# Forward and backward of a gated mix of two attentions: query blocks asked for ten steps ahead, transposing loads issued a piece later, first tiles of a stage placed over tiles that are done early

## The chip, the cores and the metric

The kernel runs on one core of one Trainium2 chip. The metric is the device time of one launch in microseconds. Five engines carry the work: TensorE (PE in the profile; PEld is its weight load), VectorE (DVE), ScalarE (ACT), GpSimd (POOL) and SyncE (SP). SP, ACT and POOL also issue DMAs, each in the order of its own instruction queue, and the transfers run on 16 DMA engines.

## The reference

The kernel computes the output of a gated mix and the gradients of its inputs. Branch A is an attention with 32 query heads over one key and value head (2048 tokens, head size 18). Branch B goes through the same tokens in 64 segments of 32; each segment attends to itself and to 8 memory rows, and its output for these rows is the memory of the next segment.

```python
def _A_ref(x, wq, wk, wv, wo):                      # S=2048, D=576, H=32, Dh=18
    q = (x @ wq).reshape(B, S, H, Dh).transpose(0, 2, 1, 3)
    k, v = x @ wk, x @ wv
    p = softmax(einsum('bhqd,bkd->bhqk', q, k) * Dh ** -0.5)
    o = einsum('bhqk,bkd->bhqd', p, v)
    return o.transpose(0, 2, 1, 3).reshape(B, S, H * Dh) @ wo

def _B_ref(x, mem0, Wq, Wk, Wv, Wo, seg_len):       # H=32, Dh=128, M=8, seg_len=32
    mem = mem0
    for s in range(S // seg_len):
        h = concatenate([mem, x[:, s * seg_len:(s + 1) * seg_len]], axis=1)
        q, k, v = (einsum('btd,dhe->bhte', h, W) for W in (Wq, Wk, Wv))
        p = softmax(where(mask, einsum('bhqe,bhke->bhqk', q, k) * scale, -1e9))
        o = einsum('bhte,hed->btd', einsum('bhqk,bhke->bhqe', p, v), Wo)
        mem = o[:, :M]
        outs.append(o[:, M:])
    return concatenate(outs, axis=1)

g = sigmoid((x * gate_w).sum(-1, keepdims=True))
out = g * A(x) + (1 - g) * B(B_x)
# returned: out and the gradients of out, for a given grad_out, to the eleven inputs A_x ... gate_w
```

All inputs and outputs are bfloat16; B_x is a constant with no gradient.

## The kernel before, in words

The program is one long sequence of stages. Everything from the forward weave on is written with an order set by hand: within an engine, instructions run in the order in which the Python code emits them. The stages, with their stretch in the profiled execution (us from the span's start):

- projections, 0 to 432;
- the forward weave, 432 to 2138: the recurrent chain of B's forward (b_chain_fwd) with the steps of A's first pass (a_pass1) between its pieces;
- b_bulk, 2138 to 2770: the token part of B's backward that doesn't hang on the recurrence;
- the backward weave, 2770 to 4426: the recurrent chain of B's backward (b_chain_bwd, 64 segments, last one first) with the first 928 steps of A's second pass (a_pass2) between its pieces;
- b_post, 4426 to 4658: what is left of B's gradient to its inputs;
- b_dw, 4658 to 5422: weight gradients, with the last 96 steps of a_pass2 among them;
- a_final, 5422 to 5529.

**weave** (L279) runs 12 steps of a_pass2 first, then one piece of the chain and one step in turn, with some extra steps behind pieces 4, 7 and 9 (counted from the chain's start). Every fourth of the first 48 steps also loads a part of the weights WT (load_WT, tile WT, 1152 KB).

**a_pass2** (L1856): one step n recomputes a tile of A's scores (mm_S: b_S from b_KV and b_QS; ex: Exp on ACT into b_E), forms b_dP on PE, multiplies on DVE (b_dS) and accumulates into b_acc. Of step n + 1, mm_S and ex are emitted in step n; the accumulation of step n is emitted in step n + 1. The queries come from the DRAM buffer qs_dram, in blocks of four steps of 200 KB (128 partitions by QSW = 800 columns); a tile b_QS holds two of them (400 KB), there are two such tiles, and in step n with n % 8 == 1 the block pair n // 8 + 1 is loaded (L1874). In the backward weave these loads are issued by SP, in b_dw by ACT. At the end of the weave's share, b_acc is put by in part_dram (by way of the tile b_pto, which shares its buffers with b_E), and b_dw fetches it as b_prt.

**b_chain_bwd** (L994): 14 pieces for each segment. Loads for the next segment to come (s - 1) are emitted in the pieces of segment s: load_a (L1013 to L1019), load_b (r_kx and r_k, L1023 and L1025), load_c (L1028, L1030), load_dT (three transposing loads into the tile r_dT, L1035), and kv_load (r_kvS, r_kvR, r_ks, r_kr, L1069 to L1077). r_pj and r_x are PSUM tiles of its projections; WoT is the transposed output weight; dm is the memory's gradient.

**b_bulk**: in each tick (137 of them) trans() transposes four heads of q, k, dO, o and v on PE into a PSUM tile x_tr (two buffers) and copies it to SBUF (x_qT, x_kT ... L768). With q and k a second transposition rides along: transp() (L723) puts half of a tile of x_dS or x_P through PE into the same x_tr (copied at L755) and the other half through DVE's own transpose (L726), giving x_DT and x_PT, which later ticks read. x_po is the product that uses them, x_b another product.

**b_post** (L1264): 50 ticks; load() fetches y_ldk and y_ldv (L1295) or y_q, y_dO, y_pd, and y_dq by a transposing load (L1304); st_T transposes on PE (y_pt) into y_T, st_H accumulates y_pdx, and y_dx holds its result before the store to dxB_dram.

**b_dw** (L1388): load_h (L1421) fetches w_h, the other operand of the weight gradients, load(k) fetches w_d, two tiles for each k (L1410, 2 MB each, with transposing loads of oh_dram at L1414), and mem_tok fetches z_src (L588) and transposes z_v. w_acc holds the products.

SBUF pools are taken from the left or from the right (RIGHT); a tile that lies over another one's place waits until that one's last reader is done. Before, a_pass2's pools a3s and a3k are taken from the right in the weave; so are wH (for w_h) and yr behind it, while ys is on the left.

## Time and profile before

| | us |
|---|---|
| time, median of 3 runs | 5536.03 |
| the 3 runs | 5531.0, 5537.22, 5536.03 |
| time of the profiled execution | 5530.78 |
| its span | 5529.1 |
| PE busy, share of the span | 5202.2, 94% |
| mean granted clock of TensorE | 0.976 of full |

One execution was profiled. Each instruction has a start, a duration and, where its engine stood idle ahead of it, what ended the idle time (its releaser). Names such as b_S<-b_KV,b_QS say which tile an instruction writes and which it reads. In a window by stretch, the granted clock is the mean share of full speed that TensorE was given. A queue of DMA issues is named SPq or ACTq.

### The profile page before, as it was taken

How to read it: one execution, taken by the hardware profiler on the slowest of the kernel's cores; microseconds unless marked ns; L12 is line 12 of the kernel's file. 1: busy time of each engine (PE TensorE's matmuls, PEld its weight loads, DVE VectorE, ACT ScalarE, POOL GpSimd, SP SyncE). 2: the span in 40 equal slices, each digit the busy share in tenths (PEclk: the TensorE clock that was granted, in tenths of full speed). 3: DMA queues.
4: the chain of work that ended last, by engine and by line, in shares of the span. 5: the costliest groups of instructions: out<-in, count | busy, mean ns of one | idle time of the engine just before them, and what ended most of it. 6: DMA issues, size and time to landing. Idle time of an engine off the chain costs nothing. (4 is left out here: it accounts for less than half of the span.)

```text
span 5529.1 us, 221015 instructions
## 1 busy us (share of the span) xinstructions
PE 5202.2 (94%) x95713; PEld 2806.3 (51%) x95713; DVE 3576.1 (65%) x7083; ACT 3308.1 (60%) x4738; POOL 2163.1 (39%) x4186
## 2 busy tenths in 40 slices
PE   8999999999999998999979999999999988999998
PEld 6434444444444445666625455445555576754444
DVE  5337888888888887656668777777777812333322
ACT  4327788787878885555657777777777712222211
POOL 4004555554555544333324445444544411121112
PEclk9999999999999999999979999999999999999999
DMA  6646766766665546888765788787877687856653
GB/s 215 219 172 135 137 137 131 136 136 132 137 131 120 119 98 183 253 246 259 228 221 153 171 175 175 175 171 178 179 178 176 141 222 197 253 189 207 185 165 103
DMA packets 1030196, 959.11 MB, mean 173 GB/s; under 512 B 596834, under 2 KB 861931, under 8 KB 1019618
## 3 DMA queue, kind: packets, MB, share of 16 engines
q1 hardware_dynamic: 921730, 687.65, 52.5%
q0 software_dynamic: 100784, 247.24, 14.7%
q8 instruction: 748, 12.26, 1.0%
q10 hardware_dynamic: 6704, 10.08, 0.7%
q14 instruction: 230, 1.88, 0.1%
HBM read 522.08 MB, written 371.33 MB: 162 GB/s over the span
## 5 line engine op out<-in xcount | busy, mean ns | idle before, releaser
L1912 DVE TENSOR_TENSOR b_dS<-b_dP,b_E 128x512 bf16<-128x512 f32 x2048 | 1314.7, 684 | 586.5 <-PE b_dP L86 256.0
L1774 DVE TENSOR_TENSOR a_W<-a_dP,a_E 128x512 bf16<-128x512 f32 x2048 | 1314.4, 684 | 276.0 <-issue 128.3
L1888 ACT ACTIVATE b_E<-b_S 128x1024 bf16<-128x1024 f32 x1024 | 1048.7, 1024 | 629.3 <-PE b_dP L86 546.3
L1744 ACT ACTIVATE a_E<-a_S 128x1024 bf16<-128x1024 f32 x1024 | 1049.9, 1025 | 254.9 <-PE a_dP L86 168.1
L86 PEld LDWEIGHTS <-b_QS 32*128 32x128 bf16 (+1 forms) x8192 | 234.5, 89 | 586.8 <-issue 517.0
L86 PE MATMUL b_S<-b_KV,b_QS 32*128 32x512 bf16 x2048 | 412.3, 396 | 106.3 <-ACT b_E L1888 60.5
L86 PE MATMUL r_pj<-WT,r_dT 128*32 128x288 bf16 x12288 | 489.9, 290 | 5.2 <-issue 5.2
L86 PE MATMUL w_acc<-w_d,w_h 128*128 128x512 bf16 (+1 forms) x2400 | 484.6, 380 | 0.0
L86 PE MATMUL a_S<-a_QD,l_KV 32*128 32x512 bf16 x2048 | 399.5, 384 | 38.6 <-ACT a_E L1744 35.1
L86 PE MATMUL b_acc<-b_dS,b_QS 128*18 128x512 bf16 x2048 | 422.5, 396 | 2.2 <-issue 1.7
L86 PE MATMUL b_dP<-b_KV,b_QS 32*128 32x512 bf16 x2048 | 412.6, 398 | 1.5 <-DVE b_dS L1912 1.5
L86 PE MATMUL a_acc<-a_W,l_WK 128*32 128x512 bf16 x4096 | 413.6, 390 | 0.3 <-DVE a_W L1774 0.2
L86 PE MATMUL b_acc<-b_E,b_QS 128*18 128x512 bf16 x2048 | 409.4, 396 | 0.6 <-issue 0.6
L86 PE MATMUL a_acc<-a_E,l_VK 128*32 128x512 bf16 x4096 | 403.8, 381 | 4.8
L86 PE MATMUL a_dP<-a_QD,l_KV 32*128 32x512 bf16 x2048 | 399.4, 386 | 0.1
L86 PEld LDWEIGHTS <-r_dT 128*32 128x32 bf16 x12288 | 324.5, 97 | 99.4 <-issue 11.6
L86 PEld LDWEIGHTS <-w_h 128*128 128x128 bf16 (+1 forms) x2688 | 224.9, 100 | 257.8 <-issue 20.6
L86 PEld LDWEIGHTS <-hm 128*32 128x32 bf16 x7680 | 204.0, 97 | 194.8 <-issue 0.7
L869 POOL TENSOR_TENSOR x_prod<-x_dOT,x_oT 128x512 bf16<-128x512 bf16 x128 | 148.0, 1156 | 300.5 <-ACT x_oT L866 278.9
L86 PEld LDWEIGHTS <-l_KV 32*128 32x128 bf16 x4096 | 121.8, 91 | 249.7 <-issue 205.0
L86 PEld LDWEIGHTS <-l_WK 128*32 128x32 bf16 x4096 | 106.7, 93 | 221.1 <-issue 220.6
L86 PE MATMUL x_b<-WoN,x_oT 128*128 128x288 bf16 x1024 | 211.3, 290 | 3.5 <-issue 3.5
(465 smaller groups left out, 10118.2 us busy)
## 6 DMA issues: line engine op xcount, KB each, us to landing
b_QS<-qs_dram SPq DMA_DIRECT2D x116, 400.0 KB
dOx_dram<-p_tok SPq DMA_DIRECT2D x16, 1024.0 KB
c_vx<-vx_dram SPq DMA_DIRECT2D x64, 256.0 KB
krow_dram<-c_k POOLq DMA_DIRECT2D x64, 256.0 KB
qrow_dram<-c_q POOLq DMA_DIRECT2D x64, 256.0 KB
vrow_dram<-c_v POOLq DMA_DIRECT2D x64, 256.0 KB
x_q<-qx_dram SPq DMA_DIRECT2D x32, 512.0 KB
x_dO<-dOx_dram SPq DMA_DIRECT2D x32, 512.0 KB
```

The costliest lines, as they stand in the source:

```text
L86: return self.nc.tensor.matmul(out, lhsT, rhs, start=start, stop=stop, tile_position=tp, skip_group_check=True)
L869: nc.gpsimd.tensor_tensor(out=sc["prod", t][:], in0=sc["dOT", t][:], in1=oT[:], op=ALU.mult)
L1744: nc.scalar.activation(E_[n][:], S.pop(n)[:], ACT.Exp, scale=SCALEA)
L1774: nc.vector.tensor_tensor(out=W_[n][:, i, :], in0=dP[i][:], in1=E_[n][:, i, :], op=ALU.mult)
L1888: nc.scalar.activation(E_[n][:], S.pop(n)[:], ACT.Exp, scale=SCALEA)
L1912: nc.vector.tensor_tensor(out=D_[n][:, i, :], in0=dP[i][:], in1=E_[n][:, i, :], op=ALU.mult)
```

## The change

1. *Query blocks.* qs_dram is laid out by blocks of four steps. A tile b_QS holds one block (200 KB) and there are four of them, so they take the same room. Three are loaded at the start, and in step n with n % 4 == 1 block n // 4 + 3 is loaded. The store of qs_dram and its readers follow the new layout.
2. *Transposing loads of the chain.* load_dT(s - 1, 2) comes after load_b and after the next yield; load_dT(s - 1, 0) after the next yield. Two pieces of a segment so hand over to a step of a_pass2 before these loads are issued, and not after.
3. *b_bulk.* The DVE transpose of a ride is issued behind the two copies that read x_tr, and no longer ahead of them.
4. *Pools.* a3s and a3k are taken from the left, between rw and rs. In b_post, y_ldk and y_ldv come from ys (left) rather than yr (right), the two y_dx tiles are taken first in ys, and load(0) of dq is emitted ahead of load(1).
5. *w_h.* load_h is a method; b_post calls it in tick 31, where b_dw called it as its first act. In the queue order before, that call's loads were issued ahead of b_post's first ones.
6. *w_d.* For k == 0 the two tiles are taken in their plain order.

```diff
@@ -723,8 +723,7 @@
         def transp(d, r, nm, pt):
             self.tr(pt[:, 4, :], d[:, 1, r, :].rearrange("p i t -> p (i t)"), P)
             o = sp.tile([P, 256], BF16, name=nm, bufs=2)
-            nc.vector.transpose(o[:, 0:128], d[:, 0, r, :].rearrange("p i t -> p (i t)"))
-            return o
+            return o, d[:, 0, r, :].rearrange("p i t -> p (i t)")
 
         def attend_m(PT, m):
             po = psum.tile([P, 4, P], F32, name="x_po", bufs=2)
@@ -752,7 +751,8 @@
             if 0 <= t < NG:
                 trans_out(t, w, nb, pt)
             if o2:
-                nc.vector.tensor_copy(o2[:, 128:256], pt[:, 4, :])
+                nc.vector.tensor_copy(o2[0][:, 128:256], pt[:, 4, :])
+                nc.vector.transpose(o2[0][:, 0:128], o2[1])
 
         def trans_out(t, w, nb, pt):
             tt, g, r, d = view(t)
@@ -772,8 +772,9 @@
             def put(pt):
                 if 0 <= t < NG:
                     tt, g, r, d = view(t)
-                    sc[out, t] = transp(d[nm], r, "x_" + out, pt)
-                    return sc[out, t]
+                    o2 = transp(d[nm], r, "x_" + out, pt)
+                    sc[out, t] = o2[0]
+                    return o2
             return put
 
         st_QT = lambda t: trans(t, "q", 2, ride(t - 8, "dS", "DT"))
@@ -1199,11 +1200,11 @@
             yield
             mem_cols(1, mem_grad("r_x", ((rows(mrow["dx"]), [perm] * 8), (rows(mrow["q"]), blk(dSqB)))))
             heads(4)
-            load_dT(s - 1, 2)
             if s:
                 load_b(s - 1, nxt)
             nc.gpsimd.dma_start(self.dTm_dram[s // 16][:, :, s % 16, :], dTc[:].rearrange("p w u c t -> p w (u c t)"))
             yield
+            load_dT(s - 1, 2)
             heads(3)
             kv_mm(n0 + 1)
             yield
@@ -1214,12 +1215,12 @@
                 pad_in("p", nxt["pT"][:, 1, :])
             yield
             heads(8)
-            load_dT(s - 1, 0)
             if s:
                 Pq = pad_T("p")
             if n1 == 0:
                 kv_load(0)
             yield
+            load_dT(s - 1, 0)
             heads(6)
             if n1 - n0 == 4:
                 kv_mm(n0 + 2)
@@ -1261,7 +1262,14 @@
         nc.vector.tensor_copy(mg[:, :, P:GD], pt[0:8, 4, 0:64].rearrange("p (g c) -> p g c", c=16))
         nc.gpsimd.dma_start(self.outs[6].rearrange("b m d -> (b m) d"), m)
 
-    def b_post(self, sp, rp, psum):
+    def load_h(self, xs, ms, wH):
+        n = self.NTT + self.NM // P
+        ht = wH.tile([P, n, D], BF16, name="w_h", bufs=1)
+        self.nc.sync.dma_start(ht[:, 0:self.NTT, :], xs.rearrange("(n p) d -> p n d", p=P))
+        self.nc.sync.dma_start(ht[:, self.NTT:n, :], ms.rearrange("(n p) d -> p n d", p=P))
+        return ht
+
+    def b_post(self, sp, rp, psum, wH):
         nc = self.nc
         NTT = self.NTT
         T0 = self.T - RIDE * (self.NSEG - KR)
@@ -1291,7 +1299,7 @@
                 names = [{"q": "dk", "dO": "dv"}.get(w, w) for w in names if w != "pd"]
             for w in names:
                 if w in ("dk", "dv"):
-                    d[w] = rp.tile([P, 8, P], BF16, name=f"y_l{w}", bufs=3)
+                    d[w] = sp.tile([P, 8, P], BF16, name=f"y_l{w}", bufs=3)
                     nc.sync.dma_start(d[w][:].rearrange("p h e -> p (h e)"),
                                       self.xtok[w][tt * P:(tt + 1) * P, h0 * P:h0 * P + 1024])
                     continue
@@ -1352,16 +1360,17 @@
                         self.mm(pdx[tt][:, hf, 0:288], lhsT=d[w][:, i, :], rhs=self.WT[wi][:, 4 * g + i, 288 * hf:288 * hf + 288],
                                 start=(g == 0 and wi == 0 and i == 0), stop=(g == 7 and wi == 2 and i == 3))
             if g == 7:
-                dx = sp.tile([P, D], BF16, name="y_dx", bufs=2)
+                dx = dxt[tt % 2]
                 nc.scalar.copy(dx[:].rearrange("p (a b) -> p a b", a=2), pdx.pop(tt)[:, :, 0:288])
                 n = min(P, T0 - tt * P)
                 nc.gpsimd.dma_start(self.dxB_dram[tt * P:tt * P + n, :], dx[0:n, :])
 
         stages = (st_KV, st_T, st_H)
+        dxt = [sp.tile([P, D], BF16, name=f"y_dx{i}") for i in range(2)]
         load(0, ("pd", "q", "dO"))
+        load(0, ("dq",))
         load_s(0)
         load(1, ("pd", "q", "dO"))
-        load(0, ("dq",))
         load(2, ("pd", "q", "dO"))
         load(1, ("dq",))
         load(2, ("dq",))
@@ -1379,6 +1388,8 @@
             for n, st in enumerate(stages):
                 if 0 <= t - n < NG:
                     st(t - n)
+                if n == 0 and t == 31:
+                    self.ht = self.load_h(self.db_dram, self.dm_dram, wH)
                 if n == 0 and t < NG:
                     if t % 2 == 1:
                         load(t // 2 + 3, ("pd", "q", "dO"))
@@ -1406,7 +1417,7 @@
             tiles = [(wB if k % 2 else wA).tile([P, n, 512], BF16, name="w_d", bufs=2) for _ in range(2)]
             for jc in (2 * jp, 2 * jp + 1):
                 cs = slice(jc * 512, (jc + 1) * 512)
-                t = tiles.pop(-1 if k == 0 else 0)
+                t = tiles.pop(0)
                 nc.sync.dma_start(t[:, 0:NTT, :], self.xtok[which][0:self.T, cs].rearrange("(n p) d -> p n d", p=P))
                 ts.append((t, cs))
                 if k < 4:
@@ -1417,12 +1428,6 @@
                 else:
                     nc.sync.dma_start(t[:, NTT:n, :], self.mtok[which][:, cs].rearrange("(n p) d -> p n d", p=P))
             return ts
-
-        def load_h(xs, ms, wH):
-            ht = wH.tile([P, n, D], BF16, name="w_h", bufs=1)
-            nc.sync.dma_start(ht[:, 0:NTT, :], xs.rearrange("(n p) d -> p n d", p=P))
-            nc.sync.dma_start(ht[:, NTT:n, :], ms.rearrange("(n p) d -> p n d", p=P))
-            return ht
 
         def groups(k, ts, ht):
             if k < 4:
@@ -1465,7 +1470,7 @@
             yield
 
         with self.tc.manual_schedule():
-            ht = load_h(self.db_dram, self.dm_dram, wH)
+            ht = self.ht
             nxt = load(0)
             wo = sp.tile([P, NKT, D], BF16, name="w_wo", bufs=1)
             nc.vector.memset(wo[64:128, 4, :], 0.0)
@@ -1482,7 +1487,7 @@
                 if k < 15:
                     nxt = load(k + 1)
                 if k == 1:
-                    hx = load_h(self.A_x, self.mem_dram, sp)
+                    hx = self.load_h(self.A_x, self.mem_dram, sp)
                 gl = self.gate_load(k, sp)
                 if k == 15:
                     for _ in sweep:
@@ -1509,7 +1514,7 @@
 
     def setup_A_dram(self, dram):
         T = self.T
-        self.qs_dram = dram.tile([NPR, 2, P, 2, QSW], BF16, name="qs_dram")
+        self.qs_dram = dram.tile([NPR, 4, P, QSW], BF16, name="qs_dram")
         self.part_dram = dram.tile([P, 512], F32, name="part_dram")
         self.kv_dram = dram.tile([P, T], BF16, name="kv_dram")
         self.vk_dram = dram.tile([2, P, self.NTT, 64], BF16, name="vk_dram")
@@ -1800,7 +1805,7 @@
         self.nc.vector.tensor_copy(dlT[:], ptr[:].rearrange("p a b -> p (a b)"))
         for i in range(2):
             r0 = 32 * (2 + i) + DA
-            self.nc.gpsimd.dma_start(self.qs_dram[:, t4 // 2, r0:r0 + 2, t4 % 2, 0:512], dlT[32 * i:32 * i + 32, :])
+            self.nc.gpsimd.dma_start(self.qs_dram[:, t4, r0:r0 + 2, 0:512], dlT[32 * i:32 * i + 32, :])
 
     def a_post(self, p, qb, acs, sp, psum, dl_all):
         nc = self.nc
@@ -1850,10 +1855,10 @@
         nc.gpsimd.tensor_tensor(out=qc[:], in0=qt[:, :, :, 0:DA],
                                 in1=rl[:].rearrange("p a b c -> p a (b c)").unsqueeze(3).to_broadcast([P, 4, 4, DA]),
                                 op=ALU.mult)
-        dq_.dma_start(self.qs_dram[p, qb // 2][:, qb % 2, 512:QSW], qc[:].rearrange("p a b c -> p (a b c)"))
+        dq_.dma_start(self.qs_dram[p, qb][:, 512:QSW], qc[:].rearrange("p a b c -> p (a b c)"))
 
     def qs_q(self, p, qb):
-        return self.qs_dram[p, qb // 2][:, qb % 2, 0:512]
+        return self.qs_dram[p, qb][:, 0:512]
 
     def a_pass2(self, keep, sp, psum, lo, hi, rd, dkp, nd):
         nc = self.nc
@@ -1869,14 +1874,14 @@
         Q, S, E_, D_ = {}, {}, {}, {}
 
         def load(c):
-            if 8 * c < hi:
-                Q[c] = sp.tile([P, 2, QSW], BF16, name="b_QS", bufs=2)
-                rd.dma_start(Q[c][:], self.qs_dram[(c // 2) % NPR, c % 2])
+            if 4 * c < hi:
+                Q[c] = sp.tile([P, QSW], BF16, name="b_QS", bufs=4)
+                rd.dma_start(Q[c][:], self.qs_dram[(c // 4) % NPR, c % 4])
 
         def mm_u(dst, n, base):
             for i in range(2):
                 r = slice(base + 32 * i, base + 32 * i + 32)
-                self.mm(dst[i], lhsT=Q[n // 8][r, n // 4 % 2, n % 4 * P:n % 4 * P + P], rhs=KV[n // NS][r, :],
+                self.mm(dst[i], lhsT=Q[n // 4][r, n % 4 * P:n % 4 * P + P], rhs=KV[n // NS][r, :],
                         tp=(base + 32 * i, 0))
 
         def mm_S(n):
@@ -1887,7 +1892,8 @@
             E_[n] = sp.tile([P, 2, 512], BF16, name="b_E", bufs=3)
             nc.scalar.activation(E_[n][:], S.pop(n)[:], ACT.Exp, scale=SCALEA)
 
-        load(lo // 8)
+        for c in range(3):
+            load(lo // 4 + c)
         part = None
         if lo % NS:
             part = sp.tile([P, 512], F32, name="b_prt", bufs=1)
@@ -1897,8 +1903,8 @@
         acc = None
         for n in range(lo, hi + 1):
             if n < hi:
-                if n % 8 == 1:
-                    load(n // 8 + 1)
+                if n % 4 == 1:
+                    load(n // 4 + 3)
                 if n % NS == NS // 2:
                     load_KV(n // NS + 1)
                 if n + 1 < hi:
@@ -1920,7 +1926,7 @@
                 src = (D_.pop(o), E_.pop(o))
                 for i4 in range(4):
                     w = 512 + 4 * DA * (o % 4) + DA * i4
-                    self.mm(acc[32 * i4:32 * i4 + DA, :], lhsT=Q[o // 8][:, o // 4 % 2, w:w + DA],
+                    self.mm(acc[32 * i4:32 * i4 + DA, :], lhsT=Q[o // 4][:, w:w + DA],
                             rhs=src[i4 // 2][:, i4 % 2, :], start=False, stop=last or o == hi - 1, tp=(0, 32 * i4))
                 if last:
                     dkv = dkp.tile([P, 4, P], BF16, name="r_kvo", bufs=2)
@@ -2111,14 +2117,14 @@
             tw = ExitStack()
             twp = tw.enter_context(SB("tw"))
             k.alloc_WT(twp)
-            with SB("a3s", RIGHT) as a3s, SB("a3k", RIGHT) as a3k, SB("rw") as rw, SB("rs") as rs, \
+            with SB("rw") as rw, SB("a3s") as a3s, SB("a3k") as a3k, SB("rs") as rs, \
                     SB("rk") as rk, SB("rv") as rv, SB("rd") as rd, PS("rp") as rp, PS("a3p") as a3p:
                 k.weave(k.b_chain_bwd(rw, rs, rd, rv, rk, rp), k.a_pass2(a3k, a3s, a3p, 0, SWEEP, nc.sync, rv, 3), 12,
                         {4: 8, 7: 6, 9: 8}, k.load_WT, 12)
             wHs = ExitStack()
             wH = wHs.enter_context(SB("wH", RIGHT))
             with SB("yr", RIGHT) as yr, SB("ys") as ys, PS("yp") as yp:
-                k.b_post(ys, yr, yp)
+                k.b_post(ys, yr, yp, wH)
             tw.close()
         with wHs, SB("wA", RIGHT) as wA, SB("wB") as wB, SB("ws") as ws:
             with SB("a4s") as a4s, PS("a4p") as a4p, PS("wp") as wp_:
```

## The prediction

> **What bounds the kernel now.** I read the page's first part, then the waits of PE, then the windows by stage.
>
> ```profile
> PE 5202.2 (94%) x95713; PEld 2806.3 (51%) x95713; DVE 3576.1 (65%) x7083; ACT 3308.1 (60%) x4738; POOL 2163.1 (39%) x4186
> ```
>
> PE is busy for 5202.2 of 5529.1 us, so only its 327 us of idle time, and the time in which it ran at a lower clock, can be gained. The waits of PE (engine and line, what it waited for: us, times, longest) name those that the diff touches:
>
> ```profile
> PE b_S L86 <- DMA b_QS<-qs_dram: 36.3, 15, 10.0
> PE y_pt L91 <- DMA y_ldk<-dkx_dram: 12.5, 1, 12.5
> PE r_x L86 <- DMA r_kr<-qx_dram: 6.0, 3, 2.5
> ```
>
> The timeline of PE places the largest (start, us, then in brackets the idle time before and its releaser):
>
> ```profile
> 2779.31 0.60 PE L86 MATMUL b_S<-b_KV,b_QS 32*128 32x512 bf16 x2 [9.96 <-DMA b_QS<-qs_dram]
> ...
> 3368.85 0.61 PE L86 MATMUL b_S<-b_KV,b_QS 32*128 32x512 bf16 x2 [3.41 <-DMA b_QS<-qs_dram]
> ...
> 4438.53 0.60 PE L91 MATMUL y_pt<-identB,y_ldk 128*128 128x128 bf16 x4 [12.53 <-DMA y_ldk<-dkx_dram]
> ...
> 4662.54 0.60 PE L86 MATMUL b_S<-b_KV,b_QS 32*128 32x512 bf16 x2 [4.75 <-DMA b_QS<-qs_dram]
> ```
>
> What a stall costs beyond its idle time stands in the windows (stretch, length, busy time of PE, PEld, DVE, ACT, POOL, then the granted clock, DMA share, GB/s). The first four are pairs of segments of the backward weave with the same work:
>
> ```profile
> 3342.24:3395.22 52.98, 48.12 (x1083) 25.16 (x1083) 38.97 (x69) 36.98 (x51) 24.27 (x44) 0.94 0.75 163
> 3395.22:3442.16 46.94, 45.31 (x1082) 24.83 (x1083) 38.97 (x69) 36.89 (x51) 24.27 (x44) 1.00 0.89 182
> 3442.16:3494.12 51.96, 47.92 (x1082) 25.10 (x1083) 39.07 (x69) 36.99 (x51) 24.21 (x44) 0.93 0.73 174
> 3540.69:3593.57 52.88, 47.62 (x1082) 25.15 (x1083) 38.89 (x69) 36.99 (x51) 24.28 (x44) 0.94 0.77 161
> 3368.07:3374.90 6.83, 6.05 (x56) 1.70 (x56) 2.73 (x5) 3.10 (x4) 1.82 (x3) 0.50 0.89 178
> 4062.00:4068.00 6.00, 4.53 (x62) 1.54 (x58) 2.50 (x5) 3.00 (x6) 2.04 (x4) 0.72 0.85 158
> 4162.00:4169.00 7.00, 4.97 (x94) 2.15 (x90) 4.12 (x9) 4.37 (x7) 2.23 (x4) 1.00 0.92 193
> 4429.60:4446.70 17.10, 7.46 (x38) 4.83 (x39) 1.69 (x4) 0.00 (x0) 0.00 (x0) 0.50 0.99 296
> ```
>
> Against the pair without a stall (46.94), the three with one take 17.00 more in all: 9.27 more idle time (length less busy time: 4.86, 4.04, 5.26 against 1.63) and 7.73 more busy time for the same matmuls. Right behind a stall the clock is 0.50 for 6.83 us; 7.73 over three such windows is 0.38 us lost per us at half clock.
>
> **The change part by part.** *Blocks of b_QS in the weave.* Of the 36.3 us, 9.96 stand at the weave's start and 4.75 behind b_post; 21.6 are left inside the weave. The timeline of SP shows why:
>
> ```profile
> 3350.29 0.38 SPq L1019 DMA_DIRECT2D r_oT<-oTm_dram  x1
> 3355.66 1.27 SPq L1035 DMA_TRANSPOSE r_dT<-dvx_dram  x1
> 3356.98 0.62 SPq L1023 DMA_DIRECT2D r_kx<-kx_dram  x1
> 3357.66 0.52 SPq L1025 DMA_DIRECT2D r_k<-krow_dram  x1
> 3358.23 0.93 SPq L1874 DMA_DIRECT2D b_QS<-qs_dram  x1
> ```
>
> SP held r_dT for 5 us, then issued load_b's two loads and b_QS at 3358.23; PE got it at 3368.85, 10.6 us later. A block is asked for six steps ahead (at n % 8 == 1, for the mm_S issued in step 8c+7). 116 blocks of eight steps are 928 steps over 1647 us (2779 to 4426), 1.77 us a step: a lead of 10.6 us. With ten steps the lead is 17.7, and 7.1 more is over the 3.41 of this stall, and over the 5.26 − 1.63 = 3.63 of the longest of the three. The moved load_dT(s-1, 2) helps by the same mechanism: load_b, and a b_QS that falls there, no longer stand behind a wait for PE; the two transposes are read only in the next segment, eight or more pieces on, so I cost their lateness at nothing, and at one segment's stall, 3 us, if that cover is gone. Price: 21.6 of idle time, 7.7 of slow clock in the three pairs, and the small stalls: the window from 4062 holds 1.47 us of idle time (6.00 − 4.53) and has clock 0.72, which is 3.4 us at half clock; the one from 4162 holds 2.03 and has 1.00. Counting three like the first, 3 × 3.4 × 0.38 gives 3.9: together 33. From below 10 (a third of the stalls), from above 21.6 × 17.00/9.27 = 39.6. I take 30, since the next latest load isn't seen beneath.
>
> In sentences that the sum can do without: the Trainium skill ("TensorE: Matmul & The Clock Gate", Part 1: The HAM clock gate) has the array fall to half rate after an idle window of about 3.4 us. By that rule the short stalls would carry no half clock, and 3.9 less would be gained; the 0.72 around 1.47 us of idle time speaks against it, the 1.00 around 2.03 for it.
>
> What it costs is issues: 116 more on SP.
>
> ```profile
> L1874 SPq DMA_DIRECT2D b_QS<-qs_dram x116: 332/382/1352, 2771.0 to 4398.7; - x116
> SPq L1035 <- PE r_pj L86: 248.6, 67, 7.3
> SPq L1874 <- PE b_acc L86: 136.5, 39, 17.0
> ```
>
> At the median 0.382 us that is 44 us, at the 0.57 between the starts of r_k and b_QS 66 us, over 64 segments 0.7 to 1.0 each. SP itself waits 248.6 us at r_dT for PE, 3.9 a segment, so I cost it at nothing; without that cover it is the 44 to 66 (a rival below). The blocks also wait for b_acc to leave a buffer, now every four steps instead of eight; behind that wait stand the chain's loads of the next pieces, and PE waits for those.
>
> The Trainium skill ("DMA: Bandwidth & Descriptors", Rules for kernel authors) wants small transfers coalesced, to 1 MiB or more at best, and the change halves 400 KB. By it the same 46 MB would take longer on the DMA engines; the DMA share of 0.75 to 0.89 in the pairs leaves room, and I put no price on it.
>
> *Weave start.* The first block is 200 KB instead of 400 and stands behind the same WT loads: at the 296 GB/s of the last window above that saves 0.7 us, so I take 1; bounds 0 and 2.
>
> *b_bulk.*
>
> ```profile
> L91 PE MATMUL x_tr<-identB,x_o 128*128 128x128 bf16 x512 | 51.6, 224 | 10.7 <-DVE x_DT L755 0.6
> ...
> 2503.09 0.30 DVE L726 STREAM_TRANSPOSE x_DT<-x_dS 128x128 bf16<-128x128 bf16 x1
> 2503.32 0.39 DVE L768 COPY x_qT<-x_tr 128x512 bf16<-128x512 bf16 x1
> 2503.62 0.21 DVE L755 COPY x_DT<-x_tr 128x128 bf16<-128x128 bf16 x1
> ```
>
> x_o goes into the PSUM buffer that the copy at 2503.62 reads last (end 2503.83). With the transpose behind both copies they start 0.23 us earlier (2503.32 − 2503.09), more than the 0.084 that each of the 128 ticks loses (10.7/128). The transposed tile is read a tick later, which hides its delay; if not, the 0.23 comes back. I take 9, short of the whole row; bounds 0 and 10.7.
>
> *b_post.* Before, w_h stood ahead of y_ldk in SP's queue:
>
> ```profile
> 4428.59 0.38 SPq L1423 DMA_DIRECT2D w_h<-db_dram  x1
> 4429.07 2.23 SPq L1295 DMA_DIRECT2D y_ldk<-dkx_dram  x1
> ...
> SPq L1423 <- DMA part_dram<-b_pto: 22.2, 1, 22.2
> ...
> 4405.77 0.39 PE L86 MATMUL r_x<-WoTt,dm 128*32 128x512 bf16 x4
> ```
>
> y_ldk took 9.46 us from issue to use. After, it is first, and its new place on the left lies over WoT, last read at 4405.77. So it can be issued near 4406 and be there by 4416, while PE works until 4426: the 12.53 go, and with them the 0.50 clock of the 8.2 us from 4438.53 to 4446.70 (× 0.38 = 3.1). I take 15.6; bounds 8 (issued only 5 us before the chain ends) and 16.2 (7.46 busy us at half clock, halved). Next late could be y_dq, a transpose now right behind y_ldk. w_h's 2.3 MB now go out at tick 31 of 50, 70 us before their use at 4675.
>
> *b_dw.*
>
> ```profile
> 4663.43 0.38 SPq L1410 DMA_DIRECT2D w_d<-ox_dram  x1
> 4685.02 0.99 SPq L588 DMA_DIRECT2D z_src<-dTm_dram  x2
> ...
> 4675.45 7.55 PE L86 MATMUL w_acc<-w_h,w_d 128*128 128x288 bf16 x47 [0.77 <-DMA w_d<-ox_dram]
> 4691.01 0.40 PE L91 MATMUL z_pt<-identB,z_v 128*128 128x128 bf16 x4 [3.21 <-DVE z_v L599]
> 4692.75 0.61 PE L91 MATMUL z_pt<-identB,z_v 128*128 128x128 bf16 x4 [1.35 <-POOL z_v L599]
> ...
> 4655.66 2.12 PE L86 MATMUL y_pdx<-WT,y_T 128*128 128x288 bf16 x16
> ...
> SPq L1410 <- DMA dxB_dram<-y_dx: 30.6, 1, 30.6
> 4663.43 11.97 DMA w_d<-ox_dram
> ```
>
> The first w_d waited for the store of y_dx; its new tile waits for the last matmul of y_pdx, 4657.78, 5.6 us sooner, and z_src behind it moves as far. That covers 0.77 and the 3.21 + 1.35, with about 1 of slow clock: 6.3. Against it w_d's 2 MB now meet the first b_QS. I take 6; bounds −10 (the 4.75 shrinks too) and +7 (b_QS lands with w_d's 11.97 us: 7.2 more than 4.75). The b_QS loads on ACT's queue become about twice as many and half as large; ACT is idle between its Exps there, so I cost them at nothing.
>
> The pool moves are only addresses. Sum: 30 + 1 + 9 + 15.6 + 6 = 61.6, and 5530.78 (the profiled execution, span 5529.1) less that is 5469. The median shown, 5536.03, lies 5.25 above that execution; for it I add 2: 5471.
>
> **The rivals.** (1) The lead isn't the matter: b_QS's 10.6 us are queueing in the DMA engines, and more, smaller loads queue longer. The DMA share up to 0.89 speaks for it, the 5 us hold at r_dT against it. The weave gives 10 rather than 30: 5491.
> (2) w_d's 2 MB delay b_QS behind b_post: +7 instead of −6, 5484. For it: both run on the same engines at 4658. Against: b_QS stays issued first or level. The Trainium skill ("DMA: Bandwidth & Descriptors", Issuing engines are not separate DMA queues) says that DMAs of different issuers interleave on the same 16 engines, which is this rival; no row of before shows the two together.
> (3) Slower: SP bounds the weave. Its holds for b_acc become twice as many, and each of the 39 new ones makes a chain load late by what r_kr cost, 2.0 (6.0/3): +78, no gain in the weave, −32 elsewhere: 5577. It decides once SP's issues and holds fill a segment of 23.5 us; the 3.9 of waiting for PE against 1.0 of new issues speak against it. Half of it is still slower than before (5538).
> (4) The change doesn't do what it says in b_post: y_ldk still comes after the chain, behind another wait. Then its 15.6 stay: 5487.
>
> **How the numbers follow.** Forecast 0.55, (1) 0.17, (2) 0.09, (3) 0.12, (4) 0.07. A measurement here can tell about 0.2%, 11 us, from no change. All but (3) are faster by more; mixtures of (1), (2) and (4), and a part of (3), land within: faster 0.83, same 0.06, slower 0.11. From below the bounds add to 39.6 + 2 + 10.7 + 16.2 + 10 = 78, or 5452; upward the range takes in (1), (2), (4) and pairs of them (5491 + 13 + 15.6 = 5520 with all three): 5450 to 5518, which leaves out (3).
>
> **What would show it.** PE's wait for b_QS in the weave falls from 21.6 to under 5, and no pair of segments is over 48. The wait for y_ldk is gone and the clock is 1.00 behind 4426. The idle time ahead of x_o falls below 2. z_pt's waits fall, and b_QS's first wait in b_dw is not over 5. A wait of PE for r_ loads above 6.0 would speak for (3); b_QS waits that keep their number, for (1).

## The result

The changed kernel takes 5471.63 us in the median of 4 runs (5468.04 to 5478.13), the kernel before 5536.62 us of 4 (5531.0 to 5555.02). The ratio is 0.9878, with a 95% interval of 0.9853 to 0.9903: faster by 1.0 to 1.5%. Measured once more (e2 below) it was 0.9847 (0.9820 to 0.9873). The forecast was 5471.

The profiled execution of after has a span of 5476.4 us (before: 5529.1) and ran for 5478.13, the longest of its four. The page's first part and the waits of PE:

```profile
PE 5171.7 (94%) x95713; PEld 2805.1 (51%) x95713; DVE 3579.9 (65%) x7083; ACT 3306.7 (60%) x4738; POOL 2163.2 (40%) x4186
...
PE b_S L86 <- DMA b_QS<-qs_dram: 18.1, 2, 9.6
PE x_po L86 <- issue: 16.1, 12, 3.2
PE x_SD L86 <- issue: 14.9, 13, 2.6
PE z_pt L91 <- DVE z_v L599: 3.6, 1, 3.6
PE z_pt L91 <- POOL z_v L599: 1.4, 1, 1.4
```

PE's busy time fell by 30.5 us with the same 95713 matmuls, and most of that is slow clock: by the clock records of the two traces TensorE stood at a granted clock of 0.50 for 272 us in before and for 209 in after, of these 118 and 54 in the chain's stretch. (At the prediction's 0.38 us lost per us at half clock, 63 us are 24.) Of 15 waits for b_QS two are left, those at the weave's start (9.6) and at b_dw's (8.5); the wait for y_ldk and those for r_kr aren't in the list any more. Waits put down to issue, which means that the profile shows nothing that PE waited for, are new near the top for b_bulk (x_po, x_SD); before they were 6.7 and 5.3.

The windows of after by stage (stretch, length, busy time of PE, PEld, DVE, ACT, POOL, granted clock, DMA share, GB/s): forward weave, b_bulk, the chain's stretch of the backward weave, b_post, b_dw to the end.

```profile
432.03:2146.62 1714.59, 1644.91 (x35005) 764.38 (x35006) 1417.59 (x2494) 1360.64 (x1792) 863.85 (x1975) 0.99 0.64 128
2146.62:2782.64 636.02, 575.83 (x14865) 426.13 (x14863) 391.76 (x1434) 358.08 (x719) 242.93 (x287) 0.97 0.82 245
2815.60:4388.86 1573.26, 1484.14 (x34356) 803.39 (x34357) 1274.25 (x2220) 1192.88 (x1607) 768.01 (x1395) 0.98 0.81 178
4388.86:4604.53 215.67, 214.44 (x3177) 169.88 (x3176) 41.27 (x115) 46.23 (x85) 31.85 (x57) 1.00 0.74 196
4604.53:5476.43 871.90, 838.74 (x5746) 436.34 (x5746) 261.89 (x474) 180.94 (x236) 181.16 (x283) 0.98 0.63 189
```

The same stretches of before, between the same instructions:

```profile
431.52:2132.66 1701.14, 1639.80 (x35006) 764.00 (x35007) 1415.88 (x2494) 1359.99 (x1792) 863.82 (x1975) 1.00 0.64 129
2132.66:2769.36 636.70, 583.62 (x14865) 423.44 (x14863) 389.67 (x1434) 357.88 (x719) 242.88 (x287) 0.97 0.82 245
2802.69:4425.99 1623.30, 1507.48 (x34355) 805.82 (x34355) 1274.17 (x2220) 1195.22 (x1607) 767.64 (x1394) 0.96 0.75 170
4425.99:4657.79 231.80, 218.04 (x3177) 171.52 (x3176) 41.49 (x115) 46.13 (x85) 32.08 (x58) 0.96 0.72 197
4657.79:5529.08 871.29, 839.56 (x5746) 437.03 (x5746) 261.84 (x474) 181.02 (x236) 181.21 (x283) 0.98 0.63 189
```

So in these two executions the chain's stretch gave 50.0 us (forecast 30), b_post 16.1 (15.6), b_bulk 0.7 (9) and b_dw −0.6 (6), and the forward weave, which the change leaves alone, took 13.5 back. The total came out as forecast because these misses cancel. The experiments ask where each is from.

SP's timeline of after, at the place where b_QS had stood behind r_dT, and SP's waits:

```profile
3350.81 0.63 SPq L1024 DMA_DIRECT2D r_kx<-kx_dram  x1
3351.88 0.33 SPq L1026 DMA_DIRECT2D r_k<-krow_dram  x1
3352.32 0.38 SPq L1879 DMA_DIRECT2D b_QS<-qs_dram  x1
3352.80 1.81 SPq L1036 DMA_TRANSPOSE r_dT<-dvx_dram  x1
...
SPq L1879 <- PE b_acc L86: 259.6, 85, 9.6
SPq L1036 <- PE r_pj L86: 45.7, 60, 2.0
SPq L1024 <- PE b_dP L86: 154.1, 61, 7.1
```

r_kx, r_k and b_QS now go out ahead of the transpose, and SP's hold there for r_pj is 45.7 us in all (before 248.6). Much of the hold has moved rather than gone: SP now waits 154.1 us at r_kx (L1024) for b_dP, where before that was 21.3. The two together fell from 269.9 to 199.8.

### The profile page after: what moved, and what is told of

Its sections match the earlier page's. It is cut to its first block, busy times and chain, and to the rows that moved or that the text cites. A ratio compares the mean times of both kernels' runs of the same rounds, so it can differ in the third digit from the quotient of the medians.

```text
span 5476.4 us, 221351 instructions
## 1 busy us (share of the span) xinstructions
PE 5171.7 (94%) x95713; PEld 2805.1 (51%) x95713; DVE 3579.9 (65%) x7083; ACT 3306.7 (60%) x4738; POOL 2163.2 (40%) x4186
```

## The experiments

Stretches in us from one profiled execution of each kernel; the ratio is to the kernel before, with its 95% interval. e1 to e4 share a chip, e5 to e8 another, e9 to e12 a third.

| kernel | forward weave | b_bulk | chain | b_post | b_dw to end | ratio |
|---|---|---|---|---|---|---|
| before (first profile) | 1701 | 636.7 | 1623.3 | 231.8 | 871.3 | |
| after (first profile) | 1715 | 636.0 | 1573.3 | 215.7 | 871.9 | 0.9878 (0.9853 to 0.9903) |
| e1 before again | 1703 | 638.6 | 1618.8 | 232.2 | 870.4 | 0.9989 (0.9973 to 1.0005) |
| e2 after again | 1699 | 633.2 | 1560.8 | 214.9 | 866.3 | 0.9847 (0.9820 to 0.9873) |
| e3 only blocks | 1695 | 634.2 | 1569.6 | 230.3 | 872.5 | 0.9912 (0.9886 to 0.9938) |
| e4 no blocks | 1690 | 628.6 | 1563.5 | 215.0 | 867.0 | 0.9866 (0.9834 to 0.9897) |
| e5 only load_dT | 1712 | 643.3 | 1581.5 | 232.9 | 871.6 | 0.9940 (0.9918 to 0.9963) |
| e6 only pools, w_h, w_d | 1712 | 645.1 | 1621.0 | 214.9 | 869.8 | 0.9977 (0.9962 to 0.9993) |
| e7 no load_dT move | 1711 | 632.2 | 1582.4 | 214.9 | 873.2 | 0.9874 (0.9840 to 0.9907) |
| e8 old lead | 1713 | 637.1 | 1567.0 | 214.9 | 867.3 | 0.9855 (0.9825 to 0.9885) |
| e9 only b_bulk | 1720 | 623.5 | 1620.2 | 235.2 | 873.1 | 0.9987 (0.9966 to 1.0007) |
| e10 twice the issues | 1722 | 644.5 | 1576.3 | 216.9 | 873.2 | 0.9888 (0.9861 to 0.9915) |
| e11 b_QS first in b_dw | 1710 | 640.1 | 1573.6 | 214.8 | 865.3 | 0.9853 (0.9827 to 0.9879) |
| e12 and z_src early | 1705 | 636.1 | 1565.9 | 214.8 | 864.0 | 0.9853 (0.9827 to 0.9879) |

**e1 and e2: the two kernels again.** No edit.

> The kernel before, once more, for the spread of each stage from one execution to the next. In the first profiles the forward weave, which the change doesn't touch, took 1701.1 us before and 1714.6 after, and PE's idle time put down to issue in b_bulk was 23.2 before and 41.7 after. Theory A (that idle time is the execution's own): here the forward weave lies somewhere in 1700 to 1715 and the issue idle of b_bulk in 20 to 45, not tied to the kernel. Theory B (the change brought it): 1701 within 3 and 23 within 5 again. Under both, the backward chain's stretch is 1623 within 10, with 20 to 24 us of waits for b_QS in it, and y_ldk is waited for 12 to 13.

> The changed kernel, once more. Theory A: the forward weave in 1700 to 1715, issue idle of b_bulk 20 to 45. Theory B: 1714 within 3 and 41 within 5 again. Under both: no wait for b_QS inside the backward chain, its stretch 1573 within 10, b_post 216 within 1, the wait for b_QS at the start of b_dw 8 to 9 and z_pt's 3.6 and 1.35 again.

The forward weave is 1703 in one and 1699 in the other, and the issue idle of b_bulk 28.7 us in e1 and 37.5 in e2. (These count waits of 0.15 us or more. In e1 to e4, some 93 matmuls of this stage have no record, and the small holes that they leave are no waits.) For the forward weave Theory B falls: the changed kernel took 1715 once and 1699 once, the latter 1 under A's band, and the 1690 to 1722 over all runs go with no edit, so the 13.5 us there are no cost of the change. For b_bulk both figures lie in A's band, but also in or within 1 of B's (18 to 28, and 36 to 46); that question is taken up under e9. e1 has 18.7 us of waits for b_QS in the chain (a little under the 20 named) and 12.6 for y_ldk. The chain of e2 took 1560.8, 2 below its band, its wait for b_QS in b_dw is 8.3 as expected, but z_pt's first wait is 0.3 and not 3.6: that one isn't fixed by the order.

**e3 and e4: the blocks alone, and all but the blocks.** e3 takes the layout and the loads of part 1 into the kernel before; e4 takes them out of the changed one:

```diff
-                Q[c] = sp.tile([P, QSW], BF16, name="b_QS", bufs=4)
-                rd.dma_start(Q[c][:], self.qs_dram[(c // 4) % NPR, c % 4])
+                Q[c] = sp.tile([P, 2, QSW], BF16, name="b_QS", bufs=2)
+                rd.dma_start(Q[c][:], self.qs_dram[(c // 2) % NPR, c % 2])
...
-                if n % 4 == 1:
-                    load(n // 4 + 3)
+                if n % 8 == 1:
+                    load(n // 8 + 1)
```

> The kernel before with the blocks of four steps, asked for ten steps ahead, as its only change. Theory L (the lead takes away the stalls and the slow clock behind them, and nothing else in the weave gains): waits for b_QS in the chain's stretch under 3, the stretch 1590 (1623 less 21.6 and less 11.6 of slow clock). Theory L2 (with the stalls gone the other stalls of the stretch go too, or lose their slow clock): 1573, as with the whole change. Theory D (most of the gain comes from the later transposing loads): at most 15 gained, 1608 or more. b_bulk, b_post and b_dw as before; total about 5490 by L, 5480 by L2, over 5510 by D.

> The changed kernel with its query blocks as before: 400 KB, six steps ahead. Theory L and L2: the stalls come back, over 15 us of waits for b_QS, the chain's stretch 1610 to 1625, total 5505 to 5520. Theory D (the later transposing loads do it): waits for b_QS under 8 and a stretch under 1590. b_post stays at 216. At the start of b_dw a block of 400 KB now meets w_d: the wait for b_QS is 8.5 or more (at the 12 us of w_d's landing at most).

Both kernels lost the stalls. The waits of PE in e4, with the old blocks and the old lead, are the two outside the chain:

```profile
PE b_S L86 <- DMA b_QS<-qs_dram: 19.3, 2, 10.3
```

e3 agrees with L2 (1569.6), and e4 with D (1563.5): each half of the change does the whole, and neither theory had room for that. Something in e4 other than the blocks takes the stalls away.

**e5 and e6: which part of e4 it is.** e5 moves only the two transposing loads (the diff shows the first; load_dT(s - 1, 0) moves likewise); e6 makes only the changes of pools, y_ldk, w_h and w_d.

```diff
-            load_dT(s - 1, 2)
             if s:
                 load_b(s - 1, nxt)
...
             yield
+            load_dT(s - 1, 2)
```

> The kernel before with the two transposing loads issued a piece later as its only change. The run without the new blocks had no stall for b_QS, so something else in the change takes them away alone. Theory O (SP's order: the block stood behind the hold at r_dT): waits for b_QS in the chain's stretch under 3, the stretch 1560 to 1575, everything else as before, total 55 under the kernel before of this call. Theory P (the place of the tiles: a3s and a3k on the left): the stalls stay, 18 to 22, the stretch 1615 to 1625.

> The kernel before with the pools, y_ldk first, w_h in tick 31 and the plain order of w_d (parts 4 to 6) as its only changes. Theory O: the stalls for b_QS stay, 18 to 22, and the chain's stretch is 1615 to 1625; Theory P: the stalls go, 1560 to 1575. Under both b_post is 215 to 216 (before 232), the first wait for b_QS in b_dw rises from 4.8 to about 9 (400 KB beside w_d), and b_dw to the end is within 2 of 871: total 15 under the kernel before by O, 65 by P.

Waits of PE and of SP in e5:

```profile
PE b_S L86 <- DMA b_QS<-qs_dram: 14.4, 2, 9.9
...
SPq L1035 <- PE r_pj L86: 52.8, 73, 2.1
```

and of PE in e6, with the chain's window and b_post's:

```profile
PE b_S L86 <- DMA b_QS<-qs_dram: 41.3, 16, 10.1
PE r_x L86 <- DMA r_kr<-qx_dram: 7.2, 4, 2.5
...
2822.25:4443.29 1621.04, 1504.15 (x34356) 805.62 (x34357) 1274.48 (x2220) 1194.38 (x1607) 767.74 (x1394) 0.97 0.77 173
4443.29:4658.19 214.90, 214.25 (x3177) 169.84 (x3176) 41.25 (x115) 46.14 (x85) 32.09 (x58) 1.00 0.74 197
```

Theory O: the order on SP alone, with blocks of 400 KB and the lead of six steps, ends the stalls, and the place of the tiles doesn't touch them (22.4 us of the 41.3 in e6 are in the chain, 0.4 over its band). e5's stretch is 1581.5, 6.5 over O's band, and its time 35 us under the kernel before measured beside it (5509.7 against 5544.7), not 55. The waits for r_kr go with it too: none in e5, 7.2 in e6, and 5.2 in e3, where only the blocks changed. e6 also gives b_post alone: 214.9, with the clock at 1.00.

The new order does two things at once. The packets of b_QS can be told apart in the traces with blocks of 400 KB (3200 bytes each, 128 for a block). In before, 15 blocks go out right behind r_kx and r_k, 14 of these with r_dT in front as well. In the median PE wants such a block 7.2 us after its issue, and it lands 7.5 us after it, at worst 10.9; the 99 others that could be followed are wanted after 10.6 and land after 3.9. In e5 the 15 blocks behind r_kx and r_k are wanted after 10.9 and land after 6.5, at worst 7.0. A stall was thus a late issue and a slow landing together, and no run separates the hold on SP from the transfers that go out just ahead of the block.

**e7 and e8: is the second remedy worth anything beside the first?** e7 is the changed kernel with load_dT in its old places, e8 the changed kernel with blocks of four steps at the old lead:

```diff
-                Q[c] = sp.tile([P, QSW], BF16, name="b_QS", bufs=4)
+                Q[c] = sp.tile([P, QSW], BF16, name="b_QS", bufs=3)
...
-        for c in range(3):
+        for c in range(2):
...
-                    load(n // 4 + 3)
+                    load(n // 4 + 2)
```

> The changed kernel with the two transposing loads back in their old places. Theory O: the lead alone suffices, as in the run with only the blocks: waits for b_QS under 1, stretch 1560 to 1575, and the time that of the changed kernel within 8. If the later loads were needed beside the lead, the stretch is over 1590.

> The changed kernel with blocks of four steps (three tiles) asked for six steps ahead, so the old lead, with the later transposing loads kept. Theory O: nothing stands in front of the blocks any more, no stall, stretch 1560 to 1575. Theory N (without the hold the lead still matters, as smaller blocks leave less in hand: at most six steps of queries are in SBUF rather than twelve): waits for b_QS over 5 and a stretch over 1580.

No stall in e8, 1567.0: with the later load_dT the lead isn't needed, and N falls. e7 has 0.3 us of waits for b_QS and 1582.4, 2 over the band, with 5.4 us of waits for r_kr. The five traces with lead and later load_dT (after, e2, e10, e11, e12) have 1561 to 1576, mean 1570; the five with one of the two (e3, e4, e5, e7, e8) 1563 to 1582, mean 1573. Beside the first remedy the second adds nothing that these traces can show.

**e9: b_bulk alone.** The kernel before with the transpose of a ride behind the copies.

> The kernel before with the DVE order of b_bulk as its only change. In the ten traces so far b_bulk took 634 to 645 us without it (mean 640, five traces) and 629 to 637 with it (mean 633, five traces), while the idle time put down to issue rose by about as much as the gap ahead of x_o fell. Theory I (PE is paced there by its own instruction stream as well, so what the buffer no longer holds up waits for instructions): the gap ahead of x_o under 2, issue idle of b_bulk 38 to 52, the stretch 630 to 638, the whole time 3 to 8 less. My forecast of 9, which no later wait takes back: 627 to 631.

The group ahead of x_o in e9, and the largest waits for issue:

```profile
L91 PE MATMUL x_tr<-identB,x_o 128*128 128x128 bf16 x512 | 51.1, 223 | 1.0 <-DVE x_PT L755 0.8
...
PE x_SD L86 <- issue: 14.7, 15, 1.8
PE x_po L86 <- issue: 10.1, 9, 2.1
```

The wait for the copy is all but gone: 1.0 us ahead of x_o, 0.8 of it for the copy into x_PT. The stretch, 623.5, is below both bands, and the issue idle, 32 us, is below Theory I's. But e12, with the same DVE order, has 636.1, and the ratio, 0.9987, doesn't exclude no gain. Over all traces b_bulk has a mean of 639.6 without the edit (five) and 634.6 with it (nine, 623.5 to 644.5): 5 us, with some 3 of uncertainty by their spread. The issue idle has a mean of 26.6 without the edit (23.0 to 31.8) and 37.5 with it (28.5 to 41.6). So it rises by 11 us with the edit, and Theory A of e1 doesn't hold here; it takes back the 10 that the gap ahead of x_o gives (mean 11.0 without, 1.3 with), as Theory I says, though e9 itself lies outside I's bands. The 5 us that the stage gains stand in PE's busy time instead (mean 583.8 without and 575.1 with the edit, in the ten traces without missing records). Why busy time falls and issue idle rises isn't shown.

**e10: SP's issues doubled once more.** Each load of b_QS goes out as two of 64 partitions.

```diff
-                rd.dma_start(Q[c][:], self.qs_dram[(c // 4) % NPR, c % 4])
+                for h in (slice(0, 64), slice(64, 128)):
+                    rd.dma_start(Q[c][h], self.qs_dram[(c // 4) % NPR, c % 4][h])
```

> The changed kernel with each load of b_QS issued as two, of 64 partitions each: 232 more issues on SP, the same bytes and the same lead. Theory O: SP has room, no stall for b_QS, the chain's stretch 1560 to 1582, the time within 8 of the changed kernel's. Theory S (SP is near its limit, the rival of the prediction that ends slower): each new issue of about 0.4 to 0.57 us comes through, the stretch is 1620 or more, the time over 50 more.

The issues of e10 on SP (minimum, median and longest in ns):

```profile
L1880 SPq DMA_DIRECT2D b_QS<-qs_dram x464: 465/582/2771, 2802.8 to 4382.6; - x155
```

464 at a median of 0.582 us are 270 us of SP's time, against 232 at 0.382, or 89, in after. The stretch is 1576.3, with one wait of 1.5 us for b_QS. 181 more us on SP cost PE about 8 in the chain (the other four with both remedies have a mean of 1568.4), not the 50 and more of Theory S: SP isn't the bound. That the whole time stays within 8 isn't shown: the ratio 0.9888 is 6 to 23 us above the changed kernel's 0.9878 and 0.9847.

**e11 and e12: the first blocks of b_dw.** e11 puts the first loads of a_pass2 on SP, ahead of w_d; e12 adds z_src behind the first part of w_d.

```diff
-                rd.dma_start(Q[c][:], self.qs_dram[(c // 4) % NPR, c % 4])
+                (nc.sync if 4 * c < lo + 12 else rd).dma_start(Q[c][:], self.qs_dram[(c // 4) % NPR, c % 4])
...
+        if lo:
+            yield
         mm_S(lo)
...
             ht = self.ht
+            next(sweep)
             nxt = load(0)
```

> The changed kernel with the first loads of a_pass2 in b_dw (b_KV, three of b_QS, b_prt) issued by SP ahead of w_d instead of by ACT beside it. Theory W (w_d's 2 MB went out ahead of b_QS and held its landing back): the first wait for b_QS in b_dw falls from 8.3 to 4 or 5, and as w_d isn't needed before the first six steps of a_pass2 are through, b_dw to the end is 3 to 4 shorter than in the changed kernel (866 to 873). If the wait has another cause it stays over 7.

> The same, and z_src's two loads issued right behind the first part of w_d, ahead of the transposing loads of oh_dram. Theory W: z_src lands before it is needed, z_pt's 3.6 and 1.35 go as well, and the slow clock behind them; b_dw to the end 8 to 10 shorter than in the changed kernel, the time 0.983 of the kernel before or less. If the transposing loads behind z_src become late instead, w_acc waits for w_d by 5 or more and the gain is lost.

SP's timeline in after at the start of b_dw, then ACT's:

```profile
4604.62 0.38 SPq L1421 DMA_DIRECT2D w_d<-ox_dram  x1
4605.06 19.26 SPq L1425 DMA_TRANSPOSE w_d<-oh_dram  x4
4624.49 0.46 SPq L1421 DMA_DIRECT2D w_d<-ox_dram  x1
4624.99 8.22 SPq L1425 DMA_TRANSPOSE w_d<-oh_dram  x4
4633.25 1.12 SPq L588 DMA_DIRECT2D z_src<-dTm_dram  x2
...
4605.20 1.65 ACTq L1879 DMA_DIRECT2D b_QS<-qs_dram  x3
```

and SP's in e11 with PE's first score of the stage:

```profile
4578.88 0.58 SPq L1872 DMA_DIRECT2D b_KV<-kv_dram  x1
4586.75 15.85 SPq L1880 DMA_DIRECT2D b_QS<-qs_dram  x3
4602.65 0.42 SPq L1901 DMA_DIRECT2D b_prt<-part_dram  x1
4604.28 0.38 SPq L1421 DMA_DIRECT2D w_d<-ox_dram  x1
...
4604.13 0.39 PE L86 MATMUL b_S<-b_KV,b_QS 32*128 32x512 bf16 x2
```

In e11 the wait is gone altogether, more than forecast: SP's queue was free to issue the first block while b_post still ran, where ACT's queue had it behind the last copy of y_dx. That w_d's 2 MB held b_QS back (Theory W) isn't shown by that alone, since the block also starts earlier; what speaks for it is the row of e6, where 400 KB beside w_d waited 8.8 us against 4.8 in e1. b_dw to the end became 865.3, 1 us under the lowest of the stage's 866 to 873; w_acc then waits 1.5 us for w_d. In e12 z_pt no longer waits (nor does it in e4 and e6, where z_src was left in its place), and w_acc waits 4.9 for w_d (2.3 for ox_dram, 2.6 for oh_dram); 864.0. Against the mean of the seven other traces with part 6 (after, e2, e4, e6, e7, e8, e10: 869.8) these are 4.5 and 5.8 us less; for e12 8 to 10 were forecast, and a ratio of 0.983 or less. Their ratio, 0.9853 both, isn't told apart from the changed kernel's 0.9847 and 0.9878. No version here beats it clearly.

## Why the prediction was right

The sign stood, and so did the total, but that it came within 1 us is luck. In the first pair the chain gave 20 us more than forecast and b_bulk and b_dw 15 less, and the forward weave happened to take 13.5. Over all traces the stages' means give 51 in the chain, 17 in b_post, 5 in b_bulk and 2 in b_dw, 75 together where I had 61.6; the two measurements of the whole gave 65 and 87 (medians). By the prediction's own steps:

- *Blocks of b_QS.* Mechanism right, place right, size short: 51 us rather than 30 (the chain's stretch has 1623.3, 1618.8, 1621.0 and 1620.2 with the stalls, mean 1620.8, and a mean of 1570 with both remedies). The step that failed is the term for slow clock: I counted 11.6 us, behind stalls for b_QS alone. In the first pair the 50.0 us are 26.7 of idle time (115.8 less 89.1, length less busy time), against 21.6 worked out, and 23.3 of busy time (1507.5 less 1484.1), against 11.6. The chain's time at clock 0.50 fell by 63.9 us, which at the prediction's 0.38 is 24.3. The windows of before show three more segments, each 28 us where an undisturbed one takes 23.5 (46.94/2):

```profile
3593.57:3621.28 27.71, 25.27 (x543) 12.89 (x545) 19.65 (x35) 18.46 (x26) 12.11 (x22) 0.88 0.67 161
3693.39:3722.90 29.51, 26.54 (x548) 13.53 (x549) 19.61 (x35) 19.15 (x27) 12.66 (x23) 0.83 0.85 149
3792.78:3821.07 28.29, 25.93 (x544) 13.35 (x546) 19.56 (x35) 18.56 (x26) 12.10 (x22) 0.88 0.75 155
...
3598.49 0.39 PE L86 MATMUL r_x<-WoT,dm 128*32 128x512 bf16 x2 [1.95 <-issue]
```

  Together they lose 15.1 us (85.51 − 70.41), with no wait for b_QS in them; they return every 100 us, as the stalls do, and in after the longest segment with this work has 26.9. Add r_kr's 6.0 and the 33 that I worked out, and it is 54. In each of the three, the last packet of the instruction queue (last section) that ended before PE went on from its longest idle time put down to issue came 11.5 to 12.7 us after the one before it, where the median is 5.8. Whether the held queue and its burst of loads delayed that packet isn't shown.
- *load_dT.* I costed it at nothing and let it help. By e5 it is a remedy by itself, worth 39 us of the stretch there (e4 and e8, which have it without the lead, are at 1563 and 1567), and it is what ends the waits for r_kr: none in e4, e5 and e8, 5.2 and 5.4 in e3 and e7. The lead of ten steps is another full remedy (e3: 51), and the two don't add up.
- *Rival (3), SP as the bound.* Dead by e10. The holds for b_acc did rise as named (39 to 85), and nobody waited for them.
- *Rival (1), queueing in the DMA engines.* Its forecast failed: the weave gave far more than 10, by e5 and e8 blocks of either size arrive at the old lead once load_dT comes later, and blocks of 200 KB don't land later than those of 400 (median 3.6 us after issue in after, 4.1 in before). But the slow landing that it put down to queueing is a part of a stall: in before the 15 blocks under e5 took 7.5 us to land where the others took 3.9. The prediction, which set the 5 us hold against it, had only the other half.
- *b_post.* 16.1 to 17.3 against 15.6: right, as e6 shows alone. y_dq wasn't late. Rival (4) didn't occur.
- *b_bulk.* The gap ahead of x_o went as forecast (0.2 us in after), the stage gave 0.7 in the first pair and 5 ± 3 over all traces rather than 9.
- *b_dw.* Wrong in size: −0.6 in the first pair, and 2.0 over all traces (871.8 without part 6, five; 869.8 with it, seven) rather than 6, between the forecast and rival (2). w_d went out at 4604.62, right behind y_pdx as worked out, and the wait for b_QS rose from 4.75 to 8.46. z_src didn't follow w_d forward: SP sat 19.26 us in the four transposing loads in front of it (11.69 before), and issued z_src 28.7 us into the stage against 27.2 before.
- *What would show it.* "No pair of segments over 48" failed: of the 45 neighbouring pairs with this work 31 were over 48 in before and 19 are in after, all but two of these under 50. "z_pt's waits fall" and "not over 5" failed with b_dw (3.6 and 1.4 against 3.2 and 1.4; 8.46). The longest pair has 50.97 at a clock of 0.93, behind a stall that isn't b_QS's: PE waited 0.80 us for r_prod at 3917.62, and the clock was 0.50 from 3917.79 for 6.83 us. A stall of 2.03 in before was followed by none (the window from 4162, clock 1.00), so the length of one stall doesn't tell its price.

```profile
3910.58:3961.55 50.97, 48.58 (x1082) 25.98 (x1084) 39.02 (x69) 36.78 (x51) 24.24 (x44) 0.93 0.77 162
```

## What to carry to other kernels

When a load lands late, read the queue that issues it: a wait in front of it, for something it doesn't need, costs every load behind it, and so can the loads that go out just ahead of it. Moving two such instructions was worth about as much here as a deeper prefetch. Sum a stall's price over whole segments against undisturbed ones, not over the waits that carry its name: the slow clock and the neighbours of the stall were more than half of it here. A load that is issued sooner competes with what was first before; ask who lands later.

## What the runs showed of the hardware that wasn't expected

PE's idle time put down to issue goes with its own instruction stream. The page of after lists that queue:

```profile
q8 instruction: 748, 12.26, 1.0%
```

748 packets of 16 KB would be 64 bytes for each of PE's 191 thousand matmuls and weight loads; by this sum I take the queue for PE's. In the trace's records all 35 idle times of 0.8 us or more that are put down to issue end 0.97 to 1.89 us after such a packet ended, while a packet comes every 7 us on average, so about one moment in eight would lie there by chance. In the unchanged forward weave such idle time is 6 us (e4) to 21 (e9), and the time at clock 0.50 is 13 us (e4) to 38 (e10). Both move its length, between 1690 and 1722 us, as much as half of the whole gain: for a stage like this a single pair of profiles can't tell a change below some 10 us.
